# Summing attention's weighted values in DRAM with accumulating transfers, in place of a running add on VectorE

## The chip, the cores and the metric

The kernel runs on one core of a Trainium2 chip. A core has a matrix engine (TensorE, PE in the profile, with PEld for its weight loads), VectorE (DVE), ScalarE (ACT), GpSimd (POOL) and SyncE (SP). Each works through its own queue of instructions in order and waits for the others by semaphores. Transfers are issued from SyncE, ScalarE or GpSimd and run on 16 shared DMA engines. The metric is the device time of one execution in microseconds; the median of three runs of the kernel before is 777.38 us (777.25 to 777.75).

## What is computed

A transformer block on a sequence of 2048 rows of width 1024, in bf16:

```python
h  = x + A(layernorm(x), wqkv, wo)
h2 = h + B(layernorm(h), w_gate, w_up, w_down)
```

A is attention with 32 heads of 32 channels. Each position attends to 8 positions only, itself and those 2, 4, ... 14 places earlier:

```python
off = jnp.arange(W) * dil                      # W, dil = 8, 2
idx = pos[:, None] - off[None, :]
logits = einsum("bhsd,bhswd->bhsw", q, kg) * scale   # kg = k at idx
attn = softmax(where(idx >= 0, logits, -1e9))
o = einsum("bhsw,bhswd->bhsd", attn, vg)             # vg = v at idx
return o @ wo
```

B is a gated feed-forward layer without a nonlinearity: `((x @ w_gate) * (x @ w_up)) @ w_down`, with an inner width of 3584.

## The kernel before, in words

The 2048 rows are worked through in four chunks of 512 (TC). For a chunk c the steps are: layernorm of x and its transpose; the q, k, v products (`qkv(c, ...)`, L394), whose results go through SBUF staging tiles `sg` to the DRAM tensors qd, kd, vd in a layout of (part of chunk, head) x channel x position; attention, which reads them back as qD, kD, vD with 128 partitions = 4 parts of the chunk x 32 heads; the output product `wo`, which adds to x giving h; layernorm of h and its transpose; the feed-forward products. For chunks 0 and 1 the feed-forward's first half is `ffn1(c, ...)`: 28 groups, each one gate product (pg), one up product (pu), two copies out of PSUM on ScalarE, and a gate product `gs*us` on VectorE (L600). The second half of chunk 0 is `ffn2(0, hf, ...)`, whose results are added to h on VectorE (L620). Chunks 2 and 3 and the second half of chunk 1 use products over sums of blocks, after 450 us.

Attention itself is done by VectorE alone, element by element. For each pair of offsets it multiplies q by the shifted k (L434) and adds up over the 32 channels (L436 to L444), giving the logits `lg`; then softmax (L449 to L469; the exponential, L454, on ScalarE) gives the weights `at`. Then, for each of four pairs of offsets, it multiplies the shifted v by the two weights (L477, two products into the two halves of `pv`), adds the halves (L482 or L485) and adds the sum to a running total in `oD` (L487). One such instruction works on 128 partitions x 4096 elements (32 channels x 128 positions). When the four pairs are done, GpSimd's queue stores oD to the DRAM tensor od (L489), and four transfers (L492) read it back transposed as oT, the stationary operand of the wo product (L515, and L835 for chunks 2 and 3). The same queue then loads vD of the next chunk (L420); qD and kD of the next chunk (L414, L415) are loaded ahead as soon as VectorE is done with the old ones.

Buffers matter here. Everything in the pool `att` has one buffer per tag: `pv` of attention's second half has the tag "prod", which `prod` of the next chunk's logits has too; oD, qD, kD, vD, oT have one buffer each. PSUM is a pool of eight banks, used in turn by all products. The feed-forward's tiles gs and us come from `t1k`, 30 buffers.

Order: the queues' order is fixed when the program is built. TensorE's products follow each other as the program text says: qkv for chunks 0 to 2, the first four column blocks of qkv(3), wo(0), the rest of qkv(3), ffn1(0), wo(1), ffn2(0) twice, ffn1(1), and then the block sums with wo(2) and wo(3). Attention is a generator that hands out its instructions piece by piece: after each one it yields an estimate of its time on VectorE (2.3 for a 4096-element product), and the class `Background` places it among TensorE's groups. Each group of 8 products is worth GROUP_US = 1.73 us of credit (times a rate of 0.98 from wo(0) on), and pieces are placed while there is credit. So an instruction that is dropped lets the later ones move ahead, in front of earlier TensorE groups and of the residual adds (L517, L620), gate products and norms (L190) which stand in VectorE's queue at fixed points of the program. `bg.finish(atts[c])` places what is left of a chunk's attention before wo(c) is recorded.

Of the kernel before, what the change touches and what calls it, by code (L numbers as in the profile page):

```python
# [8 lines left out]
BF = mybir.dt.bfloat16  # L9
# [3 lines left out]
ALU = mybir.AluOpType  # L13
# [7 lines left out]
DH = 32  # L21
# [6 lines left out]
SUB = TC // 4  # L28
# [50 lines left out]
def kernel(  # L79
# [11 lines left out]
    nc = tc.nc  # L91
# [13 lines left out]
    att = ctx.enter_context(tc.tile_pool(name="att", bufs=1))  # L105
# [14 lines left out]
    od = [dram.tile([4, H, DH, SUB], BF, name=f"od{c}") for c in range(NCH)]  # L120
# [297 lines left out]
    def load_v(c):  # L418
        vD = att.tile([128, DH, SUB + HB], BF, tag="vD", name=f"vD{c}")
        nc.gpsimd.dma_start(vD[:], vd[c].rearrange("c g d s -> (c g) d s"))  # L420
        qkv_in["v", c] = vD

    def prefetch_qk(c):
        if c in stored and ("q", c) not in qkv_in:
            load_qk(c)

    def attention(c):
        qD, kD = qkv_in["q", c], qkv_in["k", c]
        lg = att.tile([128, W, SUB], F32, tag="lg", name=f"lg{c}")
        for wp in range(W // 2):  # L430
            prod = att.tile([128, 2, DH, SUB], BF, tag="prod", name=f"prod{c}_{wp}")
            for j in range(2):
                o = HB - DIL * (2 * wp + j)
                nc.vector.tensor_tensor(prod[:, j], qD[:], kD[:, :, o:o + SUB], ALU.mult)  # L434
                yield 2.3
            nc.vector.tensor_tensor(prod[:, :, 0:16], prod[:, :, 0:16], prod[:, :, 16:32], ALU.add)  # L436
            yield 2.3
            nc.vector.tensor_tensor(prod[:, :, 0:8], prod[:, :, 0:8], prod[:, :, 8:16], ALU.add)
            yield 1.2
            t3 = att.tile([128, 2, 4, SUB], F32, tag="t3", name=f"t3{c}_{wp}")  # L440
            nc.vector.tensor_tensor(t3[:], prod[:, :, 0:4], prod[:, :, 4:8], ALU.add)
            yield 1.2
            nc.vector.tensor_tensor(t3[:, :, 0:2], t3[:, :, 0:2], t3[:, :, 2:4], ALU.add)
            nc.vector.tensor_tensor(lg[:, 2 * wp:2 * wp + 2, :], t3[:, :, 0], t3[:, :, 1], ALU.add)  # L444
            yield 1.0
        if c == 0:
            nc.vector.tensor_tensor(lg[0:32, :, 0:16], lg[0:32, :, 0:16], mask[:], ALU.add)
        tr = att.tile([128, 4, SUB], F32, tag="t3", name=f"tr{c}")
        nc.vector.tensor_tensor(tr[:], lg[:, 0:4], lg[:, 4:8], ALU.max)  # L449
        nc.vector.tensor_tensor(tr[:, 0:2], tr[:, 0:2], tr[:, 2:4], ALU.max)  # L450
        mx = att.tile([128, SUB], F32, tag="mx", name=f"mx{c}")
        nc.vector.tensor_tensor(mx[:], tr[:, 0], tr[:, 1], ALU.max)
        nc.vector.tensor_tensor(lg[:], lg[:], mx[:, None, :].to_broadcast((128, W, SUB)), ALU.subtract)
        nc.scalar.activation(lg[:], lg[:], ACTF.Exp, scale=float(DH) ** -0.5)  # L454
        yield 3.5
        tr2 = att.tile([128, 4, SUB], F32, tag="t3", name=f"trs{c}")
        nc.vector.tensor_tensor(tr2[:], lg[:, 0:4], lg[:, 4:8], ALU.add)
        nc.vector.tensor_tensor(tr2[:, 0:2], tr2[:, 0:2], tr2[:, 2:4], ALU.add)
        sm = att.tile([128, SUB], F32, tag="mx", name=f"sm{c}")
        nc.vector.tensor_tensor(sm[:], tr2[:, 0], tr2[:, 1], ALU.add)  # L460
        rs = att.tile([128, SUB], F32, tag="rs", name=f"rs{c}")
        nc.vector.reciprocal(rs[:], sm[:])
        yield 2.5
        prefetch_qk(c + 1)
        while ("v", c) not in qkv_in:
            yield "later", 1.0
        vD = qkv_in["v", c]
        at = att.tile([128, W, SUB], BF, tag="at", name=f"at{c}")
        nc.vector.tensor_tensor(at[:], lg[:], rs[:, None, :].to_broadcast((128, W, SUB)), ALU.mult)  # L469
        yield 1.2  # L470
        oD = att.tile([128, DH, SUB], BF, tag="oD", name=f"oD{c}")
        for wp in range(W // 2):
            pv = att.tile([128, 2, DH, SUB], BF, tag="prod", name=f"pv{c}_{wp}")
            for j in range(2):
                w = 2 * wp + j
                o = HB - DIL * w
                nc.vector.tensor_tensor(pv[:, j], vD[:, :, o:o + SUB],  # L477
                                        at[:, w, None, :].to_broadcast((128, DH, SUB)), ALU.mult)
                yield 2.3
            prefetch_qk(c + 1)  # L480
            if wp == 0:
                nc.vector.tensor_tensor(oD[:], pv[:, 0], pv[:, 1], ALU.add)  # L482
                yield 2.3
            else:
                nc.vector.tensor_tensor(pv[:, 0], pv[:, 0], pv[:, 1], ALU.add)  # L485
                yield 2.3
                nc.vector.tensor_tensor(oD[:], oD[:], pv[:, 0], ALU.add)  # L487
                yield 2.3
        nc.gpsimd.dma_start(od[c].rearrange("c g d s -> (c g) d s"), oD[:])  # L489
        oT = att.tile([128, KO, 4, SUB], BF, tag="oT", name=f"oT{c}")  # L490
        for cp in range(4):
            nc.gpsimd.dma_start(oT[:, :, cp, :], od[c][cp].rearrange("(hg hl) d s -> (hl d) hg s", hl=4))  # L492
        oTs[c] = oT
        while c + 1 < NCH and ("q", c + 1) not in qkv_in:
            yield "later", 1.0
            prefetch_qk(c + 1)
        if c + 1 < NCH:
            load_v(c + 1)
# [228 lines left out]
    def start_attention(c):  # L727
        stored.add(c)
        atts[c] = attention(c)
        bg.add(atts[c], bg.now + (16.0 if c == 0 else 0.0))  # L730
# [347 lines left out]
    for q in range(4):  # L1078
        dprod(ps_x[q], q, S1, fcells(t1h), True)
        p = lnp.tile([128, TC], F32, tag="ln", name=f"dp5_{q}")  # L1080
# [60 lines left out]
```

## Time and profile before

| | us |
|---|---|
| median of the runs | 777.38 |
| span of the profiled execution | 774.8 |
| TensorE busy | 768.9 |
| VectorE busy | 612.0 |
| ScalarE busy | 471.3 |
| GpSimd busy | 142.1 |
| VectorE: products with v, L477 (32 of 2286 ns) | 72.5 |
| VectorE: running add, L487 (12 of 2291 ns) | 27.5 |
| od store, from issue to landing (4 of 1 MB) | 7.6 to 9.8 |

The profile page comes from one execution and gives its span, from its first to its last instruction; no other time of that execution is recorded. The median of the runs is 2.6 us above the span, which is what lies around it. The granted TensorE clock is at full speed throughout. Attention's four value stages, from the first product with v to the end of the last running add, lie at 111.5 to 145.8, 211.6 to 248.8, 314.8 to 351.4 and 413.4 to 452.6 us; wo(0), wo(1), wo(2) start at 163.3, 287.7 and 452.6 us. A row of VectorE's timeline names start, length, engine, line, operation, what it writes and reads, and in brackets idle time before it and who ended it.

### The profile page before, as it was taken

The numbers are of one execution on the slowest core, as the hardware profiler recorded it, in microseconds if no ns is written. First come the engines' busy times: TensorE is split into PE (matmuls) and PEld (weight loads), VectorE is DVE, ScalarE is ACT, GpSimd is POOL, SyncE is SP. The second block draws the span as 40 slices with busy tenths as digits, with TensorE's granted clock in tenths as the row PEclk, the third lists the DMA queues.
The fourth block names the chain that finished last, engine by engine and source line by source line (L and its number), as shares of the span: only waits on it lengthen the run. The fifth ranks groups of instructions, "written<-read, shape, count | busy, mean of one in ns | idle before, by whom it ended". The sixth has DMA issues, their size and how long they took to land.

```text
span 774.8 us, 10428 instructions
## 1 busy us (share of the span) xinstructions
PE 768.9 (99%) x3691; PEld 353.5 (46%) x3691; DVE 612.0 (79%) x782; ACT 471.3 (61%) x1021; POOL 142.1 (18%) x152
## 2 busy tenths in 40 slices
PE   8999999999999999999999999999999999999998
PEld 6444444444444444444444444444444444444444
DVE  5629999999899999999988989985553444578863
ACT  4627534323476661975869899746677776788240
POOL 0000000010000200002000001008778687600000
PEclk9999999999999999999999999999999999999999
DMA  8998693895965868876745375644332423740001
GB/s 285 262 267 194 160 288 86 259 287 145 342 204 167 269 226 242 263 231 229 240 138 195 129 271 150 158 100 111 108 93 71 109 59 105 241 140 28 0 28 55
DMA packets 183716, 134.38 MB, mean 173 GB/s; under 512 B 81264, under 2 KB 176496, under 8 KB 181616
## 3 DMA queue, kind: packets, MB, share of 16 engines
q1 hardware_dynamic: 176912, 110.12, 49.9%
q0 software_dynamic: 3584, 22.02, 8.2%
q10 hardware_dynamic: 3168, 1.57, 0.9%
q8 instruction: 29, 0.48, 0.3%
q14 instruction: 23, 0.19, 0.1%
HBM read 104.86 MB, written 22.02 MB: 164 GB/s over the span
## 4 chain that ended last, share of the span: by engine, by line
PE 86%; DVE 9%; DMA 2%; ACT 1%; SPq 1%; issue 0%; DVEq 0%
PE ps L394 18%; PE pu L394 12%; PE pg L394 12%; PE dx L790 6%; PE pz L683 6%; PE acc L629 6%; PE py L683 6%; PE px L683 6%; PE wo L515 4%; PE pv L683 3%; PE dy L790 3%; DMA x<-in_A_x_dram 2%; DVE st L181 1%; DVE h L837 1%; PE ps L355 1%; PE ex L790 1%
## 5 line engine op out<-in xcount | busy, mean ns | idle before, releaser
L394 PE MATMUL ps<-lnT,w_qkv 128*128 128x512 bf16 x736 | 159.7, 379 | 0.2 <-ACT sg L307 0.2
L394 PEld LDWEIGHTS <-w_qkv 128*128 128x128 bf16 x736 | 71.8, 98 | 86.6 <-issue 0.7
L394 PE MATMUL pg<-lnT,w_wg 128*128 128x512 bf16 x448 | 105.8, 379 | 0.0
L394 PE MATMUL pu<-lnT,w_wu 128*128 128x512 bf16 x448 | 105.8, 379 | 0.0
L307 ACT CAST sg<-ps 128x512 bf16<-128x512 f32 x96 | 54.7, 590 | 51.3 <-PE ps L394 49.9
L477 DVE TENSOR_TENSOR pv<-vD,at 128x4096 bf16<-128x4096 bf16 x32 | 72.5, 2286 | 0.3
L434 DVE TENSOR_TENSOR prod<-qD,kD 128x4096 bf16<-128x4096 bf16 x32 | 72.3, 2284 | 0.1
L683 PEld LDWEIGHTS <-sw 128*128 128x128 f16 x448 | 43.8, 98 | 53.5 <-issue 0.9
L394 PEld LDWEIGHTS <-w_wu 128*128 128x128 bf16 x448 | 43.9, 98 | 52.8
L394 PEld LDWEIGHTS <-w_wg 128*128 128x128 bf16 x448 | 43.8, 98 | 52.7
L599 ACT CAST us<-pu 128x512 bf16<-128x512 f32 x56 | 33.2, 592 | 40.3 <-PE pu L394 39.5
L683 PE MATMUL px<-lnT,ws 128*128 128x512 bf16 x224 | 55.2, 379 | 0.0
L683 PEld LDWEIGHTS <-ws 128*128 128x128 f16 x336 | 32.9, 98 | 39.6
L629 PE MATMUL acc<-w_wd,gs 128*128 128x512 bf16 x224 | 48.5, 379 | 0.0
L489 POOL DMA_DIRECT2D od<-oD x4 | 2.2, 542 | 251.4 <-DVE oD L487 162.5
L664 POOL TENSOR_TENSOR sw<-ws 128x512 f16<-128x512 f16 x26 | 29.9, 1150 | 84.8 <-PE py L683 77.5
L185 ACT ACTIVATE rs<-mv,eps 128x1 f32<-128x1 f32 (+1 forms) x25 | 7.4, 297 | 53.5 <-DVE mv L182 48.6
L594 ACT CAST gs<-pg 128x512 bf16<-128x512 f32 x56 | 32.8, 586 | 10.7 <-PE pg L394 8.7
L436 DVE TENSOR_TENSOR prod<-prod 128x4096 bf16<-128x4096 bf16 x16 | 36.6, 2289 | 0.3
L543 ACT ACTIVATE junkd<-w_wd 128x512 bf16<-128x512 bf16 x56 | 34.3, 613 | 0.0
L629 PEld LDWEIGHTS <-gs 128*128 128x128 bf16 x224 | 21.9, 98 | 26.4
L700 ACT COPY py<-px 128x512 f32<-128x512 f32 x28 | 16.0, 570 | 26.3 <-PE px L683 26.3
(312 smaller groups left out, 1390.7 us busy)
## 6 DMA issues: line engine op xcount, KB each, us to landing
w_wg<-in_B_w_gate_dram SPq DMA_DIRECT2D x14, 1024.0 KB, 6.9
w_wu<-in_B_w_up_dram SPq DMA_DIRECT2D x14, 1024.0 KB, 5.4
w_wd<-in_B_w_down_dram SPq DMA_DIRECT2D x8, 896.0 KB, 7.7
w_pair<-in_B_w_gate_dram SPq DMA_DIRECT2D x14, 512.0 KB, 4.0
w_pair<-in_B_w_up_dram SPq DMA_DIRECT2D x14, 512.0 KB, 5.3
w_wo<-in_A_wo_dram SPq DMA_DIRECT2D x6, 1024.0 KB, 8.3
w_qkv<-in_A_wqkv_dram SPq DMA_DIRECT2D x5, 1024.0 KB, 11.0
kd<-sg SPq DMA_DIRECT2D x32, 144.0 KB, 3.3
```

What stands on the lines that cost most here:

```text
L307: nc.scalar.copy(sg[:, HB:HB + TC], ps[:])
L394: nc.tensor.matmul(ps[:], lhsT=wt[:, ko, bass.ts(j, 128)], rhs=rhs[:, ko, :], start=(ko == 0), stop=(ko == KO - 1))
L434: nc.vector.tensor_tensor(prod[:, j], qD[:], kD[:, :, o:o + SUB], ALU.mult)
L436: nc.vector.tensor_tensor(prod[:, :, 0:16], prod[:, :, 0:16], prod[:, :, 16:32], ALU.add)
L477: nc.vector.tensor_tensor(pv[:, j], vD[:, :, o:o + SUB], at[:, w, None, :].to_broadcast((128, DH, SUB)), ALU.mult)
L515: nc.tensor.matmul(ps[:], lhsT=oTs[c][:, kk, t, :], rhs=wts["wo", c, hf][:, kk, :], start=(kk == 0), stop=(kk == KO - 1))
L543: nc.scalar.activation(junk, src, ACTF.Abs, accum_out=self.l1[:, k:k + 1])
L594: nc.scalar.copy(gs[:], pg[:])
L599: nc.scalar.copy(us[:], pu[:])
L629: nc.tensor.matmul(acc[t][:], lhsT=hT[f][:, bass.ts(t, 128)], rhs=wts["wd", c, hf, b][:, j, :], start=(f == 0), stop=(f == NF - 1))
L683: nc.tensor.matmul(ps[:], lhsT=lhs[:, ko, :], rhs=rhs[:, ko, :], start=(fresh and ko == 0), stop=(ko == 3), skip_group_check=not fresh)
L790: nc.tensor.matmul(ps[:, bass.ds(lo, n)], lhsT=lhs[k][:, bass.ts(q, 128)], rhs=rhs[k][:, bass.ds(lo, n)], start=(fresh and k == 0), stop=( ...
```

## The change

Each pair's sum goes to DRAM on its own. The first pair's transfer writes od (a plain copy, `ALU.bypass`); the three others are accumulating transfers, which read od, add, and write it back. The running add is gone. `pv` is allocated once per chunk. Pairs 0 and 2 form their sum in the first half of pv, pairs 1 and 3 in oD, and the second half of pv takes each pair's second product, so that two places take turns as a source of the transfers. `max_dma_last_dim=4096` (bytes) cuts each row of 4096 elements in two, so that a transfer has 256 pieces of 4 KB. Everything else is textually the same; after.py is three lines shorter, so that later lines have numbers 3 lower.

```diff
+        pv = att.tile([128, 2, DH, SUB], BF, tag="prod", name=f"pv{c}")
         oD = att.tile([128, DH, SUB], BF, tag="oD", name=f"oD{c}")
+        odv = od[c].rearrange("c g d s -> (c g) d s")
         for wp in range(W // 2):
-            pv = att.tile([128, 2, DH, SUB], BF, tag="prod", name=f"pv{c}_{wp}")
-            for j in range(2):
+            a, b = (oD[:] if wp % 2 else pv[:, 0]), pv[:, 1]
+            for j, p in enumerate((a, b)):
                 w = 2 * wp + j
                 o = HB - DIL * w
-                nc.vector.tensor_tensor(pv[:, j], vD[:, :, o:o + SUB],
+                nc.vector.tensor_tensor(p, vD[:, :, o:o + SUB],
                                         at[:, w, None, :].to_broadcast((128, DH, SUB)), ALU.mult)
                 yield 2.3
             prefetch_qk(c + 1)
-            if wp == 0:
-                nc.vector.tensor_tensor(oD[:], pv[:, 0], pv[:, 1], ALU.add)
-                yield 2.3
-            else:
-                nc.vector.tensor_tensor(pv[:, 0], pv[:, 0], pv[:, 1], ALU.add)
-                yield 2.3
-                nc.vector.tensor_tensor(oD[:], oD[:], pv[:, 0], ALU.add)
-                yield 2.3
-        nc.gpsimd.dma_start(od[c].rearrange("c g d s -> (c g) d s"), oD[:])
+            nc.vector.tensor_tensor(a, a, b, ALU.add)
+            nc.gpsimd.dma_start(odv, a, max_dma_last_dim=4096,
+                                accum_op=ALU.bypass if wp == 0 else ALU.add)
+            yield 2.3
         oT = att.tile([128, KO, 4, SUB], BF, tag="oT", name=f"oT{c}")
         for cp in range(4):
             nc.gpsimd.dma_start(oT[:, :, cp, :], od[c][cp].rearrange("(hg hl) d s -> (hl d) hg s", hl=4))
```

## The prediction

> **What bounds the kernel now.** I read the page's busy times and its chain first, then busy time by stage, then VectorE's and GpSimd's timelines around the change, then the DMA groups.
>
> ```profile
> PE 768.9 (99%) x3691; PEld 353.5 (46%) x3691; DVE 612.0 (79%) x782; ACT 471.3 (61%) x1021; POOL 142.1 (18%) x152
> PE 86%; DVE 9%; DMA 2%; ACT 1%; SPq 1%; issue 0%; DVEq 0%
> ```
>
> TensorE sets the end: it is idle for 5.9 us of 774.8. Busy time by stage (PE, PEld, DVE, ACT, POOL, clock, DMA share, GB/s) shows how close VectorE is behind it:
>
> ```profile
> 111.00:146.00 35.00, 35.00 (x164) 15.84 (x162) 34.59 (x17) 16.58 (x54) 0.00 (x0) 1.00 0.54 135
> 146.00:191.00 45.00, 45.00 (x211) 20.38 (x209) 43.70 (x46) 13.38 (x41) 4.63 (x6) 1.00 0.82 232
> 191.00:249.00 58.00, 58.00 (x270) 26.29 (x269) 54.23 (x46) 36.32 (x68) 1.08 (x2) 1.00 0.78 242
> 249.00:292.00 43.00, 43.00 (x201) 19.53 (x200) 42.72 (x40) 26.04 (x47) 5.71 (x8) 1.00 0.77 254
> 292.00:352.00 60.00, 60.00 (x280) 27.18 (x279) 57.38 (x56) 37.61 (x122) 0.25 (x1) 1.00 0.77 231
> ```
>
> From 111 to 352 us TensorE never pauses, so time taken off VectorE there gains nothing. But VectorE is busy 232.6 of these 241 us: a wait put into its queue has almost nowhere to go. Its timeline (start, length):
>
> ```profile
> 118.34 4.49 DVE L477 TENSOR_TENSOR pv<-vD,at 128x4096 bf16<-128x4096 bf16 x2
> 122.87 2.29 DVE L485 TENSOR_TENSOR pv<-pv 128x4096 bf16<-128x4096 bf16 x1
> 125.19 2.29 DVE L487 TENSOR_TENSOR oD<-oD,pv 128x4096 bf16<-128x4096 bf16 x1
> ...
> 173.48 1.28 DVE L517 TENSOR_TENSOR h<-wo,h 128x512 bf16<-128x512 f32 x2
> ...
> 353.69 2.48 DVE L620 TENSOR_TENSOR h<-acc,h 128x512 bf16<-128x512 f32 x4
> ```
>
> One pair of offsets costs 9.2 us of VectorE, 2.3 of it the running add (L487). The last row is where VectorE's lag would stop TensorE: these adds free PSUM banks that ffn1(1) needs. PSUM has 8; ffn1(1) starts at 349.98, finds four free (6.9 us at 1.73 a group) and needs the next at 356.9. The first add is over at 354.3; counted from its start, 353.7, VectorE has 3.2 us to spare. GpSimd's timeline and the transfers:
>
> ```profile
> 146.14 0.54 POOL L489 DMA_DIRECT2D od<-oD  x1 [47.39 <-DVE oD L487]
> 154.30 3.54 POOL L492 DMA_DIRECT2D oT<-od  x4 [7.62 <-DMA od<-oD]
> ```
> ```profile
> od<-oD POOLq DMA_DIRECT2D x4, 1024.0 KB, 8.5
> q0 software_dynamic: 3584, 22.02, 8.2%
> ```
>
> The 1 MB store lands after 7.6 to 9.8 us, and the oT loads wait for it. GpSimd's queue as a whole carried 21 MiB (22.02 MB) in 0.082 x 774.8 = 63.5 us of all 16 engines, 3.0 us per MiB; the other 5.5 us of a store are fixed cost and sharing.
>
> **The Trainium skill.** "DMA: Bandwidth & Descriptors", section "SWDGE vs HWDGE vs iDMA": accumulating is for GpSimd-issued transfers only; the od store is on that queue already. Same page, "Anatomy of one DMA": about 2.0 us fixed plus bytes over 436 GB/s, an estimate of 4.4 us for 1 MiB; the trace has 8.5, the excess being the busy engines. Same page, "Rules for kernel authors": an accumulate reads its destination and writes it later, so an earlier transfer's semaphore must be awaited; the built order shows this wait, and before has only its store-then-load form (L489, L492). "Collectives: The Full Stack", "The bandwidth ceiling": an add in the DMA needs two source reads, which halves throughput while the add itself costs nothing. No transfer of before adds, so the trace can't say.
>
> **The change, part by part.** *Removed:* 12 adds of 2.29 us, 27.5 us of VectorE. Worth nothing directly, since TensorE has no idle time there; and the planner uses it to pull later attention work forward, ahead of the same TensorE groups.
>
> *Moved buffers:* after 453 us the loads of w_down into the old pv and oD buffers wait for chunk 3's transfers. Its last lands about 9 + 3X, so 49 us, after its first; between them and wo(2) lie 17 groups of 3.45 us, 58 us, so these loads come no later than now (they follow the store's landing at 462.8): nothing; at X = 20 about 10 us after wo(2) starts, as now.
>
> *Added on GpSimd and DMA:* 12 more 1 MB transfers, each about 0.5 us of issue (0.54 at L489) on a queue idle for 8 to 89 us at a time: nothing. DMA engines: at twice 3.0 us, 72 us over the span, 9% on top of 50%; hidden, as weights come through seven buffers. Within a chunk the four transfers now run one after the other: GpSimd holds each until the one before has landed.
>
> *Added waits on VectorE,* from the built order: pair 2's first product rewrites pv's first half, so waits for transfer 1; pair 3's rewrites oD, so waits for transfer 2; the next chunk's first logits product takes the prod buffer, so waits for transfer 3. Behind each stand, in order, gate products, residual adds and norms, for which ScalarE, PSUM banks and TensorE wait.
>
> Let X be one accumulate's landing time, P that of the plain first one, by chunk 7.9, 9.1, 7.6, 9.8 as the store has now. A pair is now 3 x 2.29 us, 6.9 with gaps.
> - Chunk 0: transfer 1 issues at 118.6, lands at 126.5; VectorE is there at 125.2: 1.3 us. Transfer 2 issues at 126.5; VectorE's pair takes 6.9: wait X-6.9. Transfer 3 the same: X-6.9. Sum 2X-12.5.
> - Chunk 1: two or three gate products of 0.34 lie in each pair: 1.5 + (X-7.6) + (X-7.9) = 2X-14.0.
> - Chunk 2: transfer 1 is covered by 14 us of residual adds and norms at wo(1); 2X-13.5.
> - Chunk 3: nothing but one wait of about X-7.7, and after its last pair eleven gate groups (38 us of TensorE) hold hardly any VectorE work: lag drains, no cost.
>
> Chunks 0 to 2 add 6X-40.0 ahead of the adds of row 353.69. The order moves work as well: nine running adds leave (20.9 us with gaps), and more of chunk 3's logits comes ahead of that row instead of only its first product: four products of 2.3 and two sets of sums (L436 to L444, 2.3 + 1.2 + 1.2 + 0.7 + 0.4, 5.9 with gaps), 21.2 us: +0.3. Off come the 3.2 us spare and about 2 of the 3.2 us that VectorE idles at 205 to 208 before two gate products (rows of 1.60 and 1.58), where ScalarE was held up by the exponential, which now stands earlier. **Loss = 6X - 45.**
>
> X is not in the trace. Lower bound: a plain transfer, 8.5, loss 6. If only packet time doubles: 8.5 + 3.0 = 11.5, loss 24. If all but 2 us doubles, sharing included: 2 + 2 x 6.5 = 15, loss 45. If the DMA's adder or 4 KB pieces slow it further, 20 or more, loss 75. I take the middle of the two doublings, 13.2: **34 us**. The delay first reaches TensorE at ffn1(0), which needs the norms after wo(0): chunk 0's waits, 2X-12.5, less three running adds (7.0), plus 8.2 of logits pulled ahead (two products, 4.6, and four sums of one pair, 3.6), less the 1.0 us by which the last transposed norm was early, so 2X-12.3, 14 us of the 34; the rest follows at the adds after wo(1) and ffn2(0).
>
> Sum: span 774.8 + 34 = 808.8; the runs' median lies 2.6 above the span: **811.5 us**.
>
> **Rivals.**
> *A, the accumulate costs little more than a store* (X 7.6 to 11): same mechanism, waits of 1 to 4 us; at 8.5, 783. For it: only 54 to 82% of DMA time is taken. Against: two reads.
> *B, the accumulate is slow and TensorE waits for oT itself* (X over 16.5). oT of chunk 0 now issues at 154.3 and wo(0) starts at 163.3 with its first piece due at 161 to 163, so about 1 us of slack; with the change it issues at 126.5 + 3X, a delay of 3X-28.8, which passes VectorE's 2X-12.3 at X = 16.5. At X = 20 both ways give about 75 us: 853. For it: three transfers in series, each a read, an add and a write of 1 MB. Against: nothing in before's trace is that slow.
> *C, not slower.* If X is under about 7.6 us the pair's own 6.9 us of products cover it, 6X-45 is within the 1.6 us that count as no change, and time stays at 777. It gains nothing beyond: TensorE's idle time from 54 to 520 us is 0.3 us. Against: at or below the fastest of the four stores.
> That the adds don't go is excluded: the built order has 12 fewer on VectorE and 12 more transfers.
>
> **How the numbers follow.** The forecast's band, X of 11 to 16.5, has 0.47: 798 to 832. A: 0.22, of which all but the bottom is slower. B: 0.26. C: 0.05. The range is to hold 8 in 10: from X of 8.8 (785) up to X of 21 (859), leaving C and a little of A below and the slow end of B above. What this measurement can tell from no change is 0.2%, 1.6 us. Faster: 0.01, since no idle time of TensorE can be won; same: 0.05, C and the bottom of A; slower: 0.94.
>
> **What would show it.** In the changed profile: no L487 row; 16 transfers to od with X as the median landing; VectorE waiting in three places a chunk for od, about 2X-13 us a chunk; TensorE idle where wo(0)'s norms, wo(1)'s and ffn2(0)'s adds come late, not spread over all; after 520 us all as before. Wrong if X is far from 13, if VectorE's waits are there but TensorE isn't idle (then PSUM and t1k buffers cover more than I counted), or if TensorE waits for weights (then the DMA load counts).

## The result, and the profile after

The changed kernel takes 797.75 us (median of 4 runs, 797.23 to 800.79), the kernel before on the same chip 777.32: a ratio of 1.027, 95% interval 1.0252 to 1.0288, so 20.4 us slower. The span of the profiled execution grew from 774.8 to 796.2 us, by 21.4. Busy times and the shares of the chain:

```profile
PE 771.4 (97%) x3632; PEld 354.6 (45%) x3691; DVE 586.0 (74%) x770; ACT 471.0 (59%) x1021; POOL 157.5 (20%) x164
PE 41%; DVE 11%; DMA 3%; ACT 1%; issue 1%; SPq 0%; DVEq 0%; ACTq 0%
```

VectorE is 26.0 us less busy. The shares of the chain add up to 57%, because it could be followed back only to 337.77 us, so TensorE's 41% can't be set against its 86% before. What it does show is where the wait at 375 us comes from; pieces of the chain (start, length):

```profile
337.77 11.27 DMA od<-pv
349.16 2.29 DVE prod L434
...
375.37 3.57 PE pg L394 x8
```

A transfer to od holds VectorE, and VectorE's queue leads to TensorE. TensorE's waits (what waited, on whom, us in total, times, longest):

```profile
PE pg L394 <- DVE h L617: 10.6, 1, 10.6
PE pg L394 <- DMA lnT<-ln: 2.9, 1, 2.9
PE ps L394 <- DVE h L514: 2.0, 2, 1.1
...
PE acc L626 <- DVE h L514: 0.2, 1, 0.2
```

In the kernel before, the longest wait between 54 and 520 us was 0.23. The waits shown all lie between 178 and 376 us; one more, of 0.7 us, lies at 60 us, ahead of anything that changed. Two of them are due to the residual adds after wo(0) (L514), which hold qkv(3)'s PSUM banks, then comes the transposed norm for ffn1(0) (lnT), and after ffn2(0) the residual adds (L617), which hold the banks of ffn1(1). GpSimd's timeline in chunk 0 (start, length, operation; in brackets how long its queue stood before it and for whom):

```profile
118.95 0.71 POOL L484 DMA_DIRECT2D od<-pv  x1 [19.84 <-DVE pv L483]
125.69 1.23 POOL L484 DMA_DIRECT2D od<-oD  x1 [6.03 <-DVE oD L483]
134.69 1.21 POOL L484 DMA_DIRECT2D od<-pv  x1 [7.77 <-DMA od<-oD]
144.88 1.19 POOL L484 DMA_DIRECT2D od<-oD  x1 [8.99 <-DMA od<-pv]
154.97 3.58 POOL L489 DMA_DIRECT2D oT<-od  x4 [8.90 <-DMA od<-oD]
```

Each accumulating transfer is issued when the one before has landed, so the time from its issue to the next is taken as its landing time X: 9.0, 10.2 and 10.1 us here, 9.0, 10.6 and 11.3 in chunk 1, 11.9, 11.8 and 9.5 in chunk 2; the mean of the nine is 10.4. (From issue to landing, as the list of transfers has it, they take 8.5 to 11.4, mean 9.9.) The oT loads of chunk 0 are issued at 154.97 against 154.30 before. VectorE's timeline, the rows that wait for these transfers in chunks 0 and 2, and the late adds:

```profile
134.19 2.29 DVE L479 TENSOR_TENSOR oD<-vD,at 128x4096 bf16<-128x4096 bf16 x1 [2.07 <-DMA od<-oD]
144.50 4.49 DVE L434 TENSOR_TENSOR prod<-qD,kD 128x4096 bf16<-128x4096 bf16 x2 [3.48 <-DMA od<-pv]
...
337.28 2.29 DVE L479 TENSOR_TENSOR oD<-vD,at 128x4096 bf16<-128x4096 bf16 x1 [4.94 <-DMA od<-oD]
...
349.16 2.29 DVE L434 TENSOR_TENSOR prod<-qD,kD 128x4096 bf16<-128x4096 bf16 x1 [5.06 <-DMA od<-pv]
...
374.63 2.48 DVE L617 TENSOR_TENSOR h<-acc,h 128x512 bf16<-128x512 f32 x4
```

With chunk 1's 1.72, 1.69 and 2.93, VectorE waits 21.9 us for od ahead of the last row, which stood at 353.69 before and comes 20.9 later. TensorE's timeline there, and after it the row of the kernel before that belongs to the one at 375.37, the fifth group of ffn1(1):

```profile
178.75 1.89 PE L394 MATMUL ps<-lnT,w_qkv 128*128 128x512 bf16 x7 [1.08 <-DVE h L514]
...
196.93 3.43 PE L394 MATMUL pg<-lnT,w_wg 128*128 128x512 bf16 x8 [2.86 <-DMA lnT<-ln]
200.19 1.89 PE L394 MATMUL pu<-lnT,w_wu 128*128 128x512 bf16 x8
...
362.86 1.89 PE L394 MATMUL pu<-lnT,w_wu 128*128 128x512 bf16 x8
375.37 3.57 PE L394 MATMUL pg<-lnT,w_wg 128*128 128x512 bf16 x8 [10.62 <-DVE h L617]
378.74 3.01 PE L394 MATMUL pu<-lnT,w_wu 128*128 128x512 bf16 x8
381.58 1.67 PE L394 MATMUL pg<-lnT,w_wg 128*128 128x512 bf16 x7
```
```profile
356.72 1.89 PE L394 MATMUL pg<-lnT,w_wg 128*128 128x512 bf16 x8
```

Four groups of ffn1(1) run (the row at 362.86 is the fourth), then TensorE stands still. Start to start a group takes 1.73 us; the first after the pause of 2.86 takes 3.26, the two after the pause of 10.62 take 3.37 and 2.84: 1.5 + 1.6 + 1.1 = 4.3 us more. The granted clock in these stretches (196.9 to 201.0, 375.4 to 378.7 and 378.7 to 381.6 us) is 0.61, 0.50 and 0.60. After the pause of 1.08 us nothing is slower. On TensorE's side the 21.4 us are: 15.7 of pauses between 100 and 400 us, 4.3 of lowered clock, 0.4 that wo(0) already lies later, and a rest of about 1. But the parts don't all lengthen the kernel. The fifth group of ffn1(1) starts 0.74 us after the first of the late adds does, so it is VectorE that sets its time, 18.65 us later than before. What TensorE lost ahead of it, the first 1.5 us of lowered clock too, only shortens its last pause. The 18.65 us and the 2.75 of lowered clock after that pause are the 21.4. From wo(2) on the two kernels run alike: the products px start at 529.58 before and 550.99 after, dx at 686.71 and 708.12, both 21.41 later.

### The profile page after: what moved, and what is told of

Read it like the earlier page. It is cut to its first block, busy times and chain, and to the rows that moved or that the text cites. A ratio compares the mean times of both kernels' runs of the same rounds, so it can differ in the third digit from the quotient of the medians.

```text
span 796.2 us, 10374 instructions
## 1 busy us (share of the span) xinstructions
PE 771.4 (97%) x3632; PEld 354.6 (45%) x3691; DVE 586.0 (74%) x770; ACT 471.0 (59%) x1021; POOL 157.5 (20%) x164
## 4 chain that ended last, share of the span: by engine, by line
PE 41%; DVE 11%; DMA 3%; ACT 1%; issue 1%; SPq 0%; DVEq 0%; ACTq 0%
PE dx L787 6%; PE pz L680 6%; PE py L680 6%; PE pg L394 6%; PE px L680 6%; PE pu L394 6%; PE pv L680 3%; PE dy L787 3%; DMA lx<-in_B_w_down_dram 2%; DMA od<-pv 1%; DVE prod L434 1%; DVE h L834 1%; DVE prodx L780 1%; DVE w_dn L780 1%; DVE st L181 1%
## 5 line engine op out<-in xcount | busy, mean ns | idle before, releaser
L394 PE MATMUL pg<-lnT,w_wg 128*128 128x512 bf16 x439 | 108.3, 388 | 13.9 <-DVE h L617 10.6
L479 DVE TENSOR_TENSOR pv<-vD,at 128x4096 bf16<-128x4096 bf16 x24 | 54.5, 2286 | 1.8 <-DMA od<-pv 1.7
L680 PE MATMUL px<-lnT,ws 128*128 128x512 bf16 x212 | 53.1, 379 | 0.6
L597 DVE TENSOR_TENSOR gs<-gs,us 128x512 bf16<-128x512 bf16 x56 | 23.4, 419 | 26.1 <-ACT us L596 26.0
L484 POOL DMA_DIRECT2D od<-pv x8 | 7.7, 958 | 164.6 <-DVE pv L483 128.6
L626 PEld LDWEIGHTS <-gs 128*128 128x128 bf16 x224 | 21.9, 98 | 26.8 <-issue 0.5
## 6 DMA issues: line engine op xcount, KB each, us to landing
od<-oD POOLq DMA_DIRECT2D x8, 1024.0 KB, 10.1
w_wo<-in_A_wo_dram SPq DMA_DIRECT2D x6, 1024.0 KB, 10.2
```

The lines of the kernel that those rows point to most:

```text
L394: nc.tensor.matmul(ps[:], lhsT=wt[:, ko, bass.ts(j, 128)], rhs=rhs[:, ko, :], start=(ko == 0), stop=(ko == KO - 1))
L479: nc.vector.tensor_tensor(p, vD[:, :, o:o + SUB], at[:, w, None, :].to_broadcast((128, DH, SUB)), ALU.mult)
L626: nc.tensor.matmul(acc[t][:], lhsT=hT[f][:, bass.ts(t, 128)], rhs=wts["wd", c, hf, b][:, j, :], start=(f == 0), stop=(f == NF - 1))
L680: nc.tensor.matmul(ps[:], lhsT=lhs[:, ko, :], rhs=rhs[:, ko, :], start=(fresh and ko == 0), stop=(ko == 3), skip_group_check=not fresh)
```

## Experiments

The theory after the result: VectorE's queue waits for the landing of transfers to od, its order carries the wait to adds and norms that TensorE needs, and nothing else of the change costs time. Rivals: the DMA load of twelve more transfers, oT coming late, and the changed place of the later attention work.

**Plain copies: the same transfers without the addition.**

```diff
-                                accum_op=ALU.bypass if wp == 0 else ALU.add)
+                                accum_op=ALU.bypass)
```

> All four transfers of a chunk are plain copies with the same waits and sizes, so od ends as the last pair's sum alone (the weighted values are not summed over the pairs; that part of the computation is left out). Theory (a landing in series counts, and the adding read is the small part of it): a plain copy in the second to fourth place lands in about 8.5 us instead of 10, VectorE's waits fall from 21.9 us by about 6 x 1.5, time about 787, more than half of the loss stays. Rival (the adding is what costs): plain copies land in 7 us or less, no wait of VectorE is left, time 777 to 779.

783.43 us, ratio 1.0072 (1.0056 to 1.0087), span 781.6. It falls between the two expectations. Two of the twelve runs took 778.5 and 778.7 us, the others 782.9 to 784.7; why stays open. VectorE's waits in chunks 0 to 2 fell from 21.9 to 2.5 + 2.1 + 1.5 + 2.7 = 8.8 us (the 9.8 of the later expectations have 1.0 of chunk 3 in them), and one pause of TensorE is left, in the same place (TensorE's timeline):

```profile
361.81 3.44 PE L394 MATMUL pg<-lnT,w_wg 128*128 128x512 bf16 x8 [4.56 <-DVE h L617]
```

From issue to landing, the second to fourth transfers of chunks 0 to 2 take 4.4 to 9.1 us, mean 6.9, where the accumulating ones in the same places took 8.5 to 11.4, mean 9.9. So about 14 of the 21 us come from the addition in the transfer, the rest from the wait for a landing at all. The queue's own line gives the price of the addition; that of plain copies and that of the changed kernel (packets, MB, share of 16 engines' span):

```profile
q0 software_dynamic: 7360, 34.61, 12.5%
```
```profile
q0 software_dynamic: 7360, 34.61, 16.6%
od<-pv POOLq DMA_DIRECT2D x8, 1024.0 KB, 8.8
od<-oD POOLq DMA_DIRECT2D x8, 1024.0 KB, 10.1
```

0.166 x 796.2 - 0.125 x 781.6 = 34.5 us more for 12 accumulating transfers, 2.9 us each, while a plain MiB costs (97.7 - 63.5) / 12 = 2.85 (97.7 us is the queue's time with plain copies, 63.5 that of the kernel before). The packet time doubles, as the prediction's lower estimate said, and the landing grows by about the same, 3.0 us.

**A third place, so that VectorE does not wait.** oT's buffer is free for most of this time; as a further source it lets VectorE form the next sum while two transfers are under way. The first form:

```diff
+        oE = att.tile([128, DH, SUB], BF, tag="oT", name=f"oE{c}")[:] if c < 3 else None
+        places = (oE, pv[:, 0], oD[:], oE) if c < 3 else (pv[:, 0], oD[:]) * 2
...
-            a, b = (oD[:] if wp % 2 else pv[:, 0]), pv[:, 1]
+            a, b = places[wp], pv[:, 1]
```

> The changed kernel with one more place for a pair's sum in chunks 0 to 2 (the buffer of oT, free then), so that pair sums go oT buffer, pv, oD, oT buffer. All 16 transfers, their sizes and their order one after the other stay, and VectorE's order is the changed kernel's; but no product finds its place still being read. Theory (VectorE's waits are the loss): no VectorE wait for od in chunks 0 to 2, time 777 to 779. Rival (16 MB of added traffic, or oT coming late through four landings in series): time stays above 790, TensorE waiting for oT or for weights.

790.95 us, ratio 1.0175 (1.0158 to 1.0192), where 777 to 779 was expected: a miss of my own making. VectorE no longer waits for od, but in chunk 2 the first product finds oT still in use by wo(1). VectorE's timeline, and TensorE's waits:

```profile
303.14 2.29 DVE L481 TENSOR_TENSOR oE<-vD,at 128x4096 bf16<-128x4096 bf16 x1 [16.55 <-PE wo L514]
```
```profile
PE acc L628 <- DVE h L516: 10.1, 3, 8.1
```

The adds of wo(1) stand behind that product in VectorE's queue, and ffn2(0) waits for their banks: another cause for a wait, and the same way to TensorE. In the second form chunk 2 uses oT's buffer only for its third pair:

```diff
-            a, b = (oD[:] if wp % 2 else pv[:, 0]), pv[:, 1]
+            if wp == (2 if c == 2 else 0):
+                oE = att.tile([128, DH, SUB], BF, tag="oT", name=f"oE{c}") if c < 3 else None
+            if c == 3:
+                a = oD[:] if wp % 2 else pv[:, 0]
+            elif c == 2:
+                a = (oD[:], pv[:, 0], oE[:] if wp == 2 else None, oD[:])[wp]
+            else:
+                a = (oE[:], pv[:, 0], oD[:], oE[:])[wp]
+            b = pv[:, 1]
```

> As the run with three places, but in chunk 2 the oT buffer is taken for the third pair only (order oD, pv, oT buffer, oD): there the first pair comes ahead of wo(1), which still reads oT, and VectorE waited 16.6 us for it, with TensorE 10.1 us idle behind. VectorE's order is the changed kernel's, all 16 transfers in series stay, and no product of chunks 0 to 2 waits. Theory (VectorE's waits are the loss): TensorE idle under 1 us from 54 to 460 us, time 777 to 779. Rival (added traffic, late oT): 785 or more.

778.16 us (777.33 to 779.14, 12 runs), ratio 1.001 (1.0001 to 1.0019). Busy times of this kernel, and all that TensorE waits after 100 us:

```profile
PE 765.9 (99%) x3632; PEld 353.4 (46%) x3691; DVE 585.6 (75%) x770; ACT 471.1 (61%) x1021; POOL 157.8 (20%) x164
```
```profile
PE pg L394 <- DMA lnT<-ln: 0.3, 1, 0.3
PE pv L688 <- DVE h L800: 0.2, 1, 0.2
```

All 16 transfers are there, the 12 accumulating ones too; they land no sooner than in the changed kernel (mean X 10.6), and the DMA engines are busier than in the changed kernel (0.94 of the time from 100 to 400 us, against 0.90, and 0.75 before). So the DMA load and the removed adds' place cost nothing that can be seen beyond 0.8 us, and oT is not late (its loads for chunk 0 are issued at 155.26); VectorE's waits are the whole loss. And with VectorE 26 us less busy the kernel is no faster than before.

**The landing time as the only thing changed.** Smaller pieces make the transfers slower and leave the order of every queue, and the choice of PSUM banks, as they are in the changed kernel. First 2 KB, then 512 bytes:

```diff
-            nc.gpsimd.dma_start(odv, a, max_dma_last_dim=4096,
+            nc.gpsimd.dma_start(odv, a, max_dma_last_dim=2048,
```

> The changed kernel with pieces of 2 KB in place of 4 KB in its 16 transfers to od; the order of every engine's instructions and the choice of PSUM banks stay as they are in the changed kernel, so only the landing time X differs. Theory: the loss is a function of VectorE's waits W alone. In the changed kernel W (chunks 0 to 2) was 21.9 us and TensorE's pauses 16.4, with plain copies 9.8 and 4.6; both say pauses = W - 5.4, with some 3 to 5 us of lowered clock on top. The same must hold here, and W must grow by 6 us for each us of X over 10.4. If reading and adding dominate a landing, pieces of 2 KB change X little, by 0 to 1 us: 797 to 804 us. Rival: what a piece costs dominates: X is 13 or more, W is 37 or more, 815 us or more; my prediction's sum, 34 us at 13.2, is then seen at work, plus the clock. Second rival: the pauses do not follow W, so the agreement of the two kernels was chance.

> As before with pieces of 512 bytes, 2048 to a transfer. Theory: small pieces are dear, so X is well over 10.4, between 13 and 20; W = 21.9 + 6(X - 10.4), pauses W - 5.4, loss pauses plus 3 to 6 us of lowered clock: at X = 14, 820 us; at X = 16, 832 us. Above X = 16.5 the weighted values of chunk 0 themselves (oT) must come too late for the output product, and TensorE's wait at wo(0) must name a transfer of oT and no longer VectorE's norms: this is rival B of the prediction. Rival: X stays under 12, 797 to 808 us: pieces cost nothing and the read of the destination is all of the extra time.

802.22 us, ratio 1.0325 (1.0282 to 1.0368), and 825.99 us, ratio 1.0625 (1.0592 to 1.0658). TensorE's waits with 2 KB, and with 512 bytes:

```profile
PE pg L394 <- DVE h L617: 13.5, 1, 13.5
PE pg L394 <- DMA lnT<-ln: 2.9, 1, 2.9
PE ps L394 <- DVE h L514: 2.6, 2, 1.7
PE acc L626 <- DVE h L514: 1.6, 2, 0.8
```
```profile
PE pg L394 <- DVE h L617: 18.0, 2, 16.2
PE wo L512 <- DMA oT<-od: 14.2, 1, 14.2
PE wo L512 <- ACT gs L591: 10.5, 1, 10.5
```

The four kernels, each from one profiled execution. W is the sum of VectorE's waits for od in chunks 0 to 2. "Adds" is how much later than before (353.69) the last adds of ffn2(0) start, "group" the same for the fifth group of ffn1(1) (356.72), "clock" what the lowered clock costs from there on.

| | mean X | 6X - 45 | W | adds | group | clock | growth of the span |
|---|---|---|---|---|---|---|---|
| plain copies | see above | | 8.8 | 7.4 | 5.1 | 1.7 | 6.8 |
| changed kernel | 10.4 | 17 | 21.9 | 20.9 | 18.7 | 2.8 | 21.4 |
| pieces of 2 KB | 11.0 | 21 | 27.2 | 26.5 | 24.2 | 2.8 | 27.2 |
| pieces of 512 bytes | 14.8 | 44 | 50.8 | 50.1 | 47.8 | 1.3 | 49.1 |

In all four the adds come later by W less 0.7 to 1.4 us, and the group's delay and the clock together give the growth to within 0.3 us. The prediction's 6X - 45, which is meant for the group's delay, is 2 to 4 us short. It can't be used for plain copies: it counts on every transfer taking longer than VectorE's work on a pair of offsets (6.9 us), and of these only some did. TensorE's pauses between 100 and 410 us are 4.6, 15.7, 20.6 and 43.0 us, W less 4.2 to 7.8, where both expectations had W less 5.4.

With 512 bytes the case that the prediction called B is seen: wo(0) waits 14.2 us for oT, whose loads are issued at 172.58, 18.3 later than before. A third way shows too: wo(1) waits 10.5 us for a PSUM bank that ScalarE has to empty, while ScalarE stands 21.06 us before an exponential (L454) whose input VectorE has late. Neither lengthens the kernel further, as the fifth group of ffn1(1) still waits for VectorE's adds.

**The dropped adds' place in the order kept.** The planner is told of 2.3 us for each add that has gone, so that later work isn't pulled ahead; in the second form in chunks 0 to 2 only:

```diff
+            if wp:
+                yield 2.3
```
```diff
+            if wp and c < 3:
+                yield 2.3
```

> The changed kernel, but the planner still counts 2.3 us for each dropped running add, so every other VectorE instruction keeps the place it has in the kernel before. Theory (the waits cost because the freed time was given to later attention work pulled ahead): the 20.9 us of empty slots take up nearly all of the 21.9 us of waits, 3 us are spare anyway; time 777 to 779, TensorE idle under 2 us. Rival (the waits cost wherever the order is, or the added DMA load does): time stays near 797.

> The planner counts the dropped running adds in chunks 0 to 2 only, so VectorE's order up to chunk 3 is that of the kernel before, and chunk 3's four transfers come early, as in the changed kernel. Theory: chunks 0 to 2 lose nothing (the run with all slots kept had TensorE idle under 1 us up to 447), and its loss of 8 us came from chunk 3's last transfers, for which the loads of w_down into the pv and oD buffers wait; with these early that loss goes too: 777 to 779. Rival (the loss after 455 us comes from VectorE being late at the end of ffn1(1)): 783 to 786.

785.66 us, ratio 1.0109 (1.0093 to 1.0124), and 784.35 us, ratio 1.0109 (1.0067 to 1.0151). Both miss 777 to 779. In both TensorE has no pause between 100 and 446 us, so for chunks 0 to 2 the theory held: the 20.6 us that nine adds took are then room for the waits. The loss comes behind chunk 3, in the second form in the range that its rival expectation gave (783 to 786). TensorE's waits, first form and second:

```profile
PE ev L789 <- DVE es L911: 2.5, 1, 2.5
PE pv L682 <- DVE h L794: 1.6, 2, 1.4
PE wo L834 <- ACT ep L932: 1.3, 1, 1.3
```
```profile
PE ex L789 <- DVE w_dn L770: 5.1, 1, 5.1
```

Chunk 3's attention now starts later against TensorE, and VectorE still waits in it (1.7 and 5.3 us in the first form, 1.7 and 5.6 in the second). What comes late behind it differs. In the second form it is the conversion of w_down (L770), which stands behind these waits in VectorE's queue, for the first products after ffn1(1). In the first form that conversion is nearly in time, and the longest pause comes behind a load of w_down into pv's buffer, which lands late. VectorE's timeline, and TensorE's:

```profile
470.52 1.15 DVE L770 TENSOR_SCALAR prodx<-prodx,sbd 128x3584 f16<-128x3584 bf16 x1 [4.38 <-DMA prodx<-in_B_w_down_dram]
```
```profile
476.99 3.17 PE L789 MATMUL ev<-kx,es 128*128 128x512 f16 x7 [2.50 <-DVE es L911]
```

In the changed kernel chunk 3's work had been pulled ahead, and the wait drained. The order thus decides at which end the loss comes out.

**VectorE held up on purpose in the kernel before,** by maxima of half a tile of h with itself, which change no value, ahead of the last adds of ffn2(0): 8 of them (2.77 us) or, with range(40), 40 (13.5 us).

```diff
+        if hf == 1:
+            for i in range(8):
+                late = hs[i % 4][:, 512:1024]
+                nc.vector.tensor_tensor(late, late, late, ALU.max)
```

> The kernel before, with 8 of the small VectorE operations at the same place: VectorE comes 2.7 us late there. Theory: 3.2 us are spare, so TensorE doesn't pause and the time is that of the kernel before, within 0.2%. Rival (nothing is spare): 780 or more.

> The kernel before, with 40 small VectorE operations (a maximum of a 128x512 bf16 piece with itself, in place, 0.34 us apart) ahead of the residual adds of the last half of ffn2(0): VectorE comes 13.5 us late there and nothing else changes. Theory: 3.2 us are spare, so TensorE idles 10.3 us; and its next products run at a lowered clock, as two groups after the 10.6 us pause of the changed kernel took 3.6 and 2.8 us in place of 1.73, which adds about 3 us: time 790 to 791. Rival (no cost beyond the pause): 787.7. Rival (more cover than counted): under 785.

> The same kernel as the run with a long delay before the residual adds, to have a readable profile of it: time 787 to 789. Its TensorE pause at the third gate product of ffn1(1) is to be set against the delay of 13.5 us (theory: 10.3 us of pause) and the next two groups of products against 1.73 us each (theory: about 3.6 and 2.8).

8 of them: 777.73 us, ratio 1.0004 (0.9995 to 1.0012), no time lost, as expected. But the adds come 2.6 us later, and the fifth group of ffn1(1) starts 0.2 us after its turn, so what was spare is used up. 40 of them: 788.36 in three runs (787.12 to 788.98; a fourth, the profiled one, took 3.8 ms and is not counted), ratio 1.014 (1.0124 to 1.0157). The same kernel again: 788.51, ratio 1.0141 (1.0126 to 1.0157). TensorE's timeline of the second run:

```profile
369.00 1.89 PE L394 MATMUL pg<-lnT,w_wg 128*128 128x512 bf16 x8 [0.61 <-DVE h L620]
...
419.11 3.02 PE L394 MATMUL pu<-lnT,w_wu 128*128 128x512 bf16 x8 [3.30 <-ACT us L599]
...
457.04 7.90 PE L794 MATMUL ex<-w_dn,gs 128*128 128x512 f16 x28 [3.28 <-DVE w_dn L775]
```

The 788.4 us lie below the 790 to 791 of the theory, and near the 787.7 of the rival without a lowered clock; yet neither sum was at work. Ten groups of ffn1(1) ran before the adds were needed, not four, and the delay came out 50 and 90 us later. The built order tells why. Which bank a group gets is settled when the program is built. In the kernel before and in the changed one, the first eight groups of ffn1(1) take banks that VectorE's adds empty, four from the first half of ffn2(0) and four from the last; here, with the maxima known, only the first four do, and the next six take banks that ScalarE has emptied. So this run does not test the count of four; the changed kernel does (the rows from 357.68 to 375.37, of which the fourth group is shown above). Here a delay that the builder knew was in part planned around; the landing of the transfers was not, as the banks in the changed kernel are those of the kernel before.

## Why the prediction was right or wrong

*Right: the mechanism and its places.* VectorE waits for transfers in two or three places a chunk, and TensorE pauses after wo(0) and at ffn2(0)'s last adds; the kernel with a third place shows that nothing else counts. One place was missed: qkv(3) waits for wo(0)'s adds before ffn1(0) waits for the norms, 2.0 of the 4.9 us there. wo(1)'s adds cost only 0.2 us.

*Mis-sized: X, at 13.2 against 10.4.* That the time lies in the stated range is owed to the width of that range. By its X the case that occurred is the one I called A (7.6 to 11), with 0.22, and not the forecast's band from 11; the runs' median, 797.75, lies just under that band's 798. Of the two doublings, "if only packet time doubles" was right in its added part (3.0 forecast; 2.9 measured in engine time, 3.0 in landing) and started from too long a base: 8.5 us is the store's landing before, while these transfers without addition land in 6.9 on average. What makes a landing long stays open: busy engines alone don't, as two plain ones in chunk 1 took 4.4 and 9.1 us while the DMA engines were equally busy (0.83). That "all but 2 us doubles" has no support. At X = 10.4 the sum gives 17 us, and the fifth group of ffn1(1) is 18.7 late.

*Left out: the clock.* I reckoned a pause at its own length. TensorE's clock is lowered after some pauses, for 4.3 us in all, of which only the 2.75 after the last pause lengthen the kernel. The Trainium skill has this ("TensorE: Matmul & The Clock Gate", "Part 1: The HAM clock gate (the "warmup" mystery)": half clock after an idle window of about 3.4 us, and about as long a time of work to come back). The trace agrees on half clock (0.50 after the pause of 10.62). On the time to come back it agrees after the pause of 2.86: at half clock, 1.5 us lost are 3 us of work; after that of 10.62 it was longer, 5.5 us for 2.75 lost. On the idle window the runs differ: a pause of 2.86 was enough, and so was that of 2.50 in the first run with the slot kept (0.50 in the 3 us after it), while after 1.81 in the run with 512 bytes the clock was 1.00. The errors had opposite signs: X takes 17 us off the 34 forecast, and the clock gives 2.75 back and the spare time, below, 0.9.

*Right: the parts costed at nothing.* The removed adds are worth nothing while TensorE is never idle: the kernel with a third place saves them and stays at 778.16. The DMA load and the issues are hidden (same run). Chunk 3's waits drained in this order, and from wo(2) on the offset stays at 21.41 us; the two runs with the slot kept show that this was owed to work pulled ahead, which the prediction had said without its condition.

*Small terms.* The first wait of chunk 0, put at 1.3 us, did not occur, as the plain copy landed before VectorE came to it. At ffn2(0)'s adds four groups ran before the pause, as counted, but 2.3 us were spare, not 3.2: I counted from the start of the first add, and the group that needs the bank starts 0.74 us after that, once the add is done. The logits pulled ahead add up to 21.0, not 21.2. Case B set in below its stated point: at a mean X of 15.4 in chunk 0 (13.4, 15.5, 17.2), not at 16.5. There 126.5 + 3X - 154.3 gives 18.3 us for the delay of oT's loads, as measured. TensorE paused for 14.2 of them, so oT had 4 us to spare, not the 1 that 3X - 28.8 allows. And the comparison with VectorE's 2X - 12.3, at 18.4, was not the one to make, since wo(0)'s pause comes first and hides the later one.

## What to carry to other kernels

When a transfer takes over part of an engine's work, ask first who rewrites its source: that instruction waits a whole landing, and everything queued behind it waits too, whether or not it has to do with the transfer. Count places against transfers under way and give one more place than can be in flight, in a buffer that is really free at that time. Time taken off an engine that isn't the bound buys nothing, and a pause of the bound costs more than its length where the clock falls after it. Of several pauses with one cause, the last sets the loss: the earlier ones only shorten it.

## What the runs showed of the hardware

- An accumulating transfer of 1 MB (bf16, pieces of 4 KB) landed 8.5 to 11.4 us after its issue, mean 9.9 over chunks 0 to 2, where plain ones in the same places took 4.4 to 9.1, mean 6.9; it takes twice the engines' time (5.7 against 2.85 us of all 16) and 1.2 us of GpSimd's issue against 0.7.
- Pieces of 512 bytes cost 4.4 us of X, with an issue of 2.1 us. With 2 KB X was 0.6 us longer and the issue 1.3; as one profiled execution stands behind each mean, so small a difference in X is not certain.
- TensorE's first groups after pauses of 2.50 us and more ran at about half clock, which cost 1.3 to 2.8 us for one pause; after single pauses of 1.08 to 1.81 us the clock was 1.00.
